# Attention scores of two head pairs in one visit of the matrix engine

## The chip, the cores and the metric

The kernel runs on one core of a Trainium2 chip. A core has a matrix engine (PE, TensorE), which also loads its stationary operands (PEld in the profile), a vector engine (DVE), an activation engine (ACT), a general engine (POOL) and a queue engine (SP). They run side by side and wait for one another by semaphores. [...] The metric is the device time of one run in microseconds (us). The kernel before took 494.76 us, the median of 3 runs (494.73 to 494.86).

## The reference

Attention over pooled keys and values feeds a small mixture of four experts. Eight batches of eight heads have 576 queries of 64 values each; eight neighbouring keys (and values) are averaged, so 72 remain.

```python
k_p = k.reshape(B, H, Sp, 8, D).mean(axis=3)          # Sp = 72
v_p = v.reshape(B, H, Sp, 8, D).mean(axis=3)
scores = scale * np.matmul(q, k_p.transpose(0, 1, 3, 2))
attn = exp(scores - max); attn /= attn.sum(-1)
x = np.matmul(attn, v_p)                              # -> rows of 512 values, one per query
for e in range(4):
    out += p[:, e] * (relu(x @ w1[e]) @ w2[e])         # 512 -> 1024 -> 512
```

Most of the arithmetic is in the last line: 4608 rows through four pairs of 512 x 1024 and 1024 x 512 products.

## The kernel before

**Chunks and tiles.** The first 512 queries of each batch make a chunk; the 64 left over from each of the eight batches make a ninth. A chunk and an expert make a tile. Chunk 0 is worked in a hand-written opening (`first_chunk`); the other 32 tiles run in one loop.

**Products.** The two expert products are not done by the textbook's eight block products of 2 x 2 blocks but by seven (sums and differences of blocks are formed on DVE ahead). `up_product` (line 642) does one of the seven of `x @ w1` for one of two halves of the hidden columns, called units; `down` (line 711) does one of the seven of `h @ w2`. A unit owns two PSUM banks. By the table at line 647, products 0, 2, 3 and 5 of a unit go to its bank 0, and products 1, 4 and 6 to its bank 1. Product 0 is also copied by ACT from bank 0 into bank 1 (line 673), where product 1 is added to it; the ReLU at line 677 then reads bank 1. From there until product 4, which starts a new sum, bank 1 is not used. Products 2 and 3 are copied by ACT from bank 0 to `partial` (line 675) before the next product is added on to bank 0. Products 4 and 6 are finished by DVE (line 640), and product 5 by ACT (line 681).

**The loop's slots.** The loop at line 1019 counts slots `g`. A slot issues, in this order: product `i` of unit 0; product `i - 1` of unit 1; the down product `i - 1` of the tile before; and then the attention pieces that were put at this slot. So each slot has 4 + 4 + 8 matrix products of 256 columns. The order written in the program is the order on each engine: nothing is rescheduled.

**The attention pieces.** While chunk `c` of the loop runs, the attention of a later batch is prepared. `pieces_later` (line 923) lists which piece stands after which slot; a batch has 28 slots, counted from the start of its four tiles. For the usual batch (3 to 7) the four `scores` pieces stand after slots -1, 3, 5 and 6, and for batch 2 (`plans[BUSY]`) after 11, 12, 13 and 15; batch 1 has its four in `first_chunk`. The `context` pieces (scores times values) come from slot 11 on (16 on for batch 2).

`scores` (line 363) works a pair of heads: four products, each with 64 contracted rows. The halves of the rows lie on partitions 0 to 63 and 64 to 127, so two of the products can run in the two halves of the matrix engine's rows at the same time, each into a bank of its own of the two-bank tile `att`. Then one ACT instruction takes the exponent of both banks, 72 x 1024 values (line 377). Batches below 2 alternate between `att` and a second tile, `att_first`, which is given up before the loop and becomes unit 0's banks. `rem_scores` (line 457) does the same for the 64 left-over queries, with 64-column products.

**Queues.** In the loop, ACT carries the copies and ReLUs of the up products, the exponents, the copy of the first down product (line 736), the scaling for POOL's additions (line 740), and for expert 0 also the first additions to the result (line 802). DVE carries the other additions (line 804), the block sums and the context's division. SP issues the transposing loads (queries, keys, context) and the stores.

Of the kernel before, what the change touches and what calls it, by code (L numbers as in the profile page):

```python
# [9 lines left out]
ACT = mybir.ActivationFunctionType  # L10
# [7 lines left out]
def kernel(  # L18
# [10 lines left out]
    nc = tc.nc  # L29
# [330 lines left out]

        return state[("kpT", b)][:].rearrange("p h j -> p (h j)")[lo:lo + D, h * SPT:h * SPT + P]

    def scores(b, pair):
        qT = state[("qT", b)]
        if pair == 0:
            state[("expT", b)] = apool.tile([SP, H, 2, 2, P], BF16, name="expT")
        expT = state[("expT", b)]
        sc_ps = two_banks(b)[:].rearrange("p a (h n) -> p a h n", h=2)
        for hh in range(2):
            h = 2 * pair + hh  # L370
            for r2 in range(2):
                lo = r2 * D
                nc.tensor.matmul(  # L373
                    sc_ps[:, r2, hh], lhsT=key_columns(b, h, lo), rhs=qT[lo:lo + D, h],
                    skip_group_check=True,
                )
        nc.scalar.activation(
            out=expT[:, 2 * pair:2 * pair + 2].rearrange("j h a b t -> j b (h a) t"),
            in_=sc_ps[0:SP].rearrange("j b h (a t) -> j b (h a) t", t=P),
            func=ACT.Exp, scale=EXP_SCALE,  # L380
        )

    def divide(c_ps, x_tok):

# [446 lines left out]
    def first_chunk():  # L831


        def each(*pieces):
            for piece in pieces:
                piece()

        sums = {e: first_weight_sums(e) for e in range(E)}

        def both(step):  # L840
            for unit in range(2):
                up_product(0, 2, unit, step)

        each(*(lambda n=n: x_sum(0, n) for n in range(4)), *sums[0][0:3])
        norm_probs()
        up(0, 1, (0, 1))
        hidden_sums(0, 0, 0)
        hidden_sums(0, 0, 1)
        up(0, 1, (2, 3))
        each(*sums[1][0:3])  # L850
        up(0, 1, (4,), bank=att_first[1][:, 1])
        each(sums[2][0], sums[2][1], sums[2][3], sums[2][2])
        up(0, 1, (5,), bank=chains[0])
        both(0)
        up(0, 1, (6,), bank=chains[1])
        both(1)
        up(0, 1, (7,), bank=chains[0])
        each(sums[0][3], sums[1][3], *weight_sums(0))
        both(2)
        down(0, 0, 0)  # L860
        hidden_sums(0, 0, 2)
        both(3)
        down(0, 0, 1)
        hidden_sums(0, 0, 3)
        both(4)
        down(0, 0, 2)
        both(5)
        down(0, 0, 3)
        both(6)
        load_w2(3)  # L870
        fold_keys(1)
        up(0, 3, (0,), bank=units[1][0])
        down(0, 0, 4)
        up(0, 3, (1, 2, 3))
        queries(1, 0)
        queries(1, 1)
        down(0, 0, 5)
        keys(1, every)
        queries(1, 2)
        down(0, 0, 6)  # L880
        scores(1, 0)
        queries(1, 3)
        turn_of("att", 2)
        up(0, 3, (4,))
        each(*sums[3][0:3])
        scores(1, 1)
        up(0, 3, (5,))
        scores(1, 2)
        up(0, 3, (6,))
        each(*weight_sums(1)[0:3])  # L890
        scores(1, 3)
        up(0, 3, (7,))
        fold_first, *fold_rest = values_folds(1)
        fold_first()
        down_plain(0, 1, 0)
        each(*fold_rest)
        load_wide(0, 0)
        load_q(2)
        load_wide(0, 1)
        load_wide(1, 0)  # L900
        load_wide(1, 1)
        load_q_rem(0)
        load_q_rem(1)
        load_wide(1, 2)
        down_plain(0, 1, 1)
        down_plain(0, 1, 2, range(0, 3))
        context(1, 0)
        down_plain(0, 1, 2, range(3, FCH))
        context(1, 1)
        turn(1, 0)  # L910
        down_plain(0, 1, 3)
        context(1, 2)
        turn(1, 1)
        down_plain(0, 2, 0)
        context(1, 3)
        turn(1, 2)
        down_plain(0, 2, 1)
        turn(1, 3)
        each(*weight_sums(3)[0:3])
        down_plain(0, 2, 2)  # L920
        each(*(lambda n=n: x_sum(1, n) for n in range(4)))

    def pieces_later():


        at = {}

        def put(slot, *pieces):
            at.setdefault(slot, []).extend(pieces)

        usual = dict(
            queries=-8, keys=-9, values=-2, scores=(-1, 3, 5, 6), contexts=(11, 14, 18, 21),
            q=1, k=(-2, 0, 5, 9), v=(-2, 0, 5, 9), x=(22, 25, 25, 25), rem=(-3, 17, 24, 25),
        )
        plans = {b: usual for b in range(BUSY, B + 1)}
        plans[BUSY] = dict(
            queries=0, keys=4, values=12, scores=(11, 12, 13, 15), contexts=(16, 18, 19, 21),
            q=6, k=(5, 8, 11, 14), v=(13, 16, 19, 26), x=(24, 25, 25, 25), rem=(0, 6, 8, 14),
        )
        plans[B] = dict(usual, x=(24, 24, 25, 25), rem=(-3, 17, 21, 22))  # L940
        plans[BUSY + 1] = dict(usual, keys=-8, values=4, v=(5, 8, 12, 16))

        for b, plan in plans.items():
            start = 7 * E * (b - BUSY)

            def put_each(what, pieces):
                for slot, piece in zip(plan[what], pieces, strict=True):
                    put(start + slot, piece)

            if b == BUSY:  # L950
                put(start + 1, lambda: fold_wide(0, 0))
                put(start + 4, lambda: fold_wide(0, 1))
                put(start + 5, lambda: load_q_rem(BUSY))
                put(start + 8, lambda: fold_wide(1, 0))
                put(start + 12, lambda: fold_wide(1, 1))
            if b < B:
                put(start + plan["queries"], lambda b=b: queries(b))
                put(start + plan["keys"], lambda b=b: fold_keys(b))
                put(start + plan["keys"] + (b > BUSY), lambda b=b: keys(b, every))
                put(start + plan["values"], *values_folds(b))  # L960
                put_each("scores", [lambda b=b, pair=pair: scores(b, pair) for pair in range(NPAIR)])

                for r, slot in zip((2, 3, 0, 1), plan["contexts"]):
                    put(start + slot, lambda b=b, r=r: context(b, r))
                    put(start + slot + 1, lambda b=b, r=r: turn(b, r))
            if b + 1 < B:
                put(start + plan["q"], lambda b=b: load_q(b + 1), lambda b=b: load_q_rem(b + 1))
                for what in range(2):
                    put_each("kv"[what], [lambda b=b, what=what, part=part: load_part(b + 1, what, part)
                                          for part in range(NR)])  # L970
            if b % 2 == 0:
                i = b // 2 - 1
                put_each("rem", [lambda i=i, do=do: do(i)
                                 for do in (rem_queries, rem_scores, rem_context, rem_turn)])
            put_each("x", [lambda b=b, n=n: x_sum(b, n) for n in range(4)])
        return at

    ENG = mybir.EngineType
    with tc.manual_schedule(
# [28 lines left out]


        N = len(order)  # L1010
        later = pieces_later()
        below_of = [(0, 3)] + order
        sums = {}
        for at, pieces in (((3,), weight_sums(3)[3:]), ((8,), weight_sums(1)[3:]), ((12, 15, 22, 14), weight_sums(2)),
                           ((15,), first_weight_sums(3)[3:])):
            for slot, piece in zip(at, pieces, strict=True):
                sums.setdefault(slot, []).append(piece)
        POOLED = (4,)
        for g in range(7 * N + 1):
            t, i = divmod(g, 7)  # L1020
            if i in (0, 2, 3) and t < N:
                hidden_sums(*below_of[t], i)
            if t < N:
                up_product(*order[t], 0, i)
            t2, i2 = divmod(g - 1, 7)
            if 0 <= t2 < N:
                up_product(*order[t2], 1, i2)
            if i == 1 and t < N:
                hidden_sums(*below_of[t], i)
            if g == 0:  # L1030

                down_plain(0, 2, NR - 1)
            else:
                down(*below_of[t2], i2, t2 % 2, POOLED)
            for piece in later.get(g, ()):
                piece()
            for piece in sums.get(g, ()):
                piece()
            if g == 7 * (N - 2):
                load_last_weights()  # L1040
# [29 lines left out]
```

## Time and profile before

| | |
|---|---|
| time, median of 3 runs | 494.76 us (494.73 to 494.86) |
| profiled execution | 494.84 us, of which 492.7 us from the first to the last instruction |
| granted clock of the matrix engine | 0.999 |
| PE busy | 485.5 us |
| PE weight loads | 408.4 us |
| DVE busy | 378.4 us |
| ACT busy | 305.5 us |
| POOL busy | 115.7 us |
| score products of `scores` | 112, in 28 visits of 4 |
| exponent of one pair, 72 x 1024 | 1020 ns |

The profile has one line per kind of instruction: its line of the kernel, the engine, what it writes and reads, how many there were, their total and mean time, and the idle time ahead of them with what ended it. [...] In a timeline each line has the start, the length, and how many equal instructions were merged into it.

### The profile page before, as it was taken

What the parts mean: (1) busy time and instruction counts of PE and PEld (TensorE: products, weight loads), DVE (VectorE), ACT (ScalarE), POOL (GpSimd) and SP (SyncE); (2) the same over time, 40 slices, a digit from 0 to 9 for tenths busy, and PEclk for the clock granted to TensorE, in tenths of its full rate; (3) what the DMA queues carried; (4) which work ended last, traced back from release to release, by engine and by line L of the source; (5) the groups of instructions that cost most, each with busy time, mean ns of one, the idle gap of its engine ahead of it and who ended that gap; (6) DMA issues with size and microseconds to landing.
All of it is one profiled execution on the core that took longest, in us unless ns stands there. A gap on an engine that the chain in (4) does not pass through costs nothing.

```text
span 492.7 us, 11536 instructions
## 1 busy us (share of the span) xinstructions
PE 485.5 (99%) x4695; PEld 408.4 (83%) x4701; DVE 378.4 (77%) x758; ACT 305.5 (62%) x569; POOL 115.7 (23%) x114
## 2 busy tenths in 40 slices
PE   8999999999999999999999999999999999999996
PEld 4867468788888888888889889888898888888885
DVE  5786889799668976798579876896678766876674
ACT  4876446856766568656765676557665566556650
POOL 8320323242432055015321352111011100010010
PEclk9999999999999999999999999999999999999999
DMA  9999999975887479344954397311111010004003
GB/s 199 212 206 203 197 172 127 107 79 69 98 118 63 79 77 144 35 79 44 162 59 84 31 151 76 68 26 44 56 23 23 23 65 1 13 21 86 1 1 87
DMA packets 101812, 41.97 MB, mean 85 GB/s; under 512 B 73840, under 2 KB 100208, under 8 KB 101760
## 3 DMA queue, kind: packets, MB, share of 16 engines
q0 software_dynamic: 56928, 22.42, 40.3%
q1 hardware_dynamic: 43728, 17.77, 16.5%
q10 hardware_dynamic: 1104, 1.05, 0.6%
q8 instruction: 37, 0.61, 0.5%
q14 instruction: 15, 0.12, 0.1%
HBM read 45.69 MB, written 9.44 MB: 112 GB/s over the span
## 4 chain that ended last, share of the span: by engine, by line
PE 98%; DVE 0%; ACT 0%; issue 0%
PE o_ps L728 41%; PE unit L660 41%; PE o_ps L754 3%; PE unit L582 2%; PE att L373 2%; PE att L427 1%; PE unit L787 1%; PE unit L326 1%; PE o_ps L582 1%; PE unit L597 1%; PE att_first L660 1%; PE o_ps L597 0%; PE att L481 0%; PE att L464 0%; PE unit L306 0%; PE att L353 0%
## 5 line engine op out<-in xcount | busy, mean ns | idle before, releaser
L804 DVE SCALAR_TENSOR_TENSOR acc<-o_ps,p_all,acc 128x256 f32<-128x256 f32 (+1 forms) x285 | 127.1, 486 | 52.6 <-PE o_ps L728 36.6
L728 PEld LDWEIGHTS <-H 128*128 128x128 bf16 x1320 | 129.0, 98 | 15.6 <-DMA w_bf<-in_moe_w_dram 0.6
L660 PEld LDWEIGHTS <-w_bf 128*128 128x128 bf16 x1056 | 100.9, 98 | 15.8 <-issue 3.6
L640 DVE CUSTOM_DVE_ANT_0 H<-unit,partial 128x512 bf16<-128x512 f32 x128 | 87.3, 685 | 26.1 <-PE unit L660 21.5
L728 PE MATMUL o_ps<-w_bf,H 128*128 128x256 bf16 x792 | 102.6, 273 | 0.3 <-ACT w_bf L675 0.3
L660 PE MATMUL unit<-xT,w_bf 128*128 128x256 bf16 x680 | 97.6, 273 | 0.0
L675 ACT COPY partial<-unit 128x512 f32<-128x512 f32 x128 | 72.0, 590 | 33.2 <-PE unit L660 33.0
L742 POOL TENSOR_TENSOR acc<-acc,addend 128x512 f32<-128x512 f32 x24 | 30.4, 1267 | 261.9 <-ACT addend L740 206.5
L660 PEld LDWEIGHTS <-wu_bf 128*128 128x128 bf16 x792 | 75.7, 98 | 10.7 <-issue 1.7
L660 PE MATMUL unit<-xs,wu_bf 128*128 128x256 bf16 x512 | 76.9, 273 | 0.0
L728 PE MATMUL o_ps<-wt_bf,H 128*128 128x256 bf16 x528 | 68.4, 273 | 0.0
L728 PEld LDWEIGHTS <-S 128*128 128x128 bf16 x528 | 51.7, 98 | 6.2
L681 ACT ACTIVATE H<-unit 128x512 bf16<-128x512 f32 x64 | 38.2, 597 | 29.5 <-PE unit L660 29.3
L677 ACT ACTIVATE H<-unit 128x512 bf16<-128x512 f32 x64 | 38.8, 606 | 27.9 <-PE unit L660 27.8
L673 ACT COPY unit<-unit 128x512 f32<-128x512 f32 x65 | 38.0, 584 | 15.4 <-PE unit L660 15.4
L660 PE MATMUL unit<-xs,w_bf 128*128 128x256 bf16 x256 | 38.5, 273 | 0.0
L802 ACT ACTIVATE acc<-o_ps,p_all 128x256 f32<-128x256 f32 x72 | 30.3, 473 | 11.0 <-PE o_ps L728 9.6
L151 POOL DMA_DIRECT2D kraw<-in_k_dram x20 | 26.4, 1319 | 37.2 <-DMA kraw<-in_k_dram 37.2
L660 PE MATMUL unit<-xT,wu_bf 128*128 128x256 bf16 x228 | 34.2, 272 | 0.0
L728 PE MATMUL o_ps<-w_bf,S 128*128 128x256 bf16 x264 | 34.2, 273 | 0.0
L728 PE MATMUL o_ps<-wt_bf,S 128*128 128x256 bf16 x264 | 34.2, 273 | 0.0
L151 POOL DMA_DIRECT2D vraw<-in_v_dram x20 | 29.2, 1462 | 17.6 <-DMA vraw<-in_v_dram 17.6
(168 smaller groups left out, 516.2 us busy)
## 6 DMA issues: line engine op xcount, KB each, us to landing
out_dram<-acc SPq DMA_DIRECT2D x32, 256.0 KB, 4.2
w_bf<-in_moe_w_dram POOLq DMA_DIRECT2D x7, 1024.0 KB, 21.9
q_sb<-in_q_dram POOLq DMA_DIRECT2D x7, 512.0 KB, 9.8
vraw<-in_v_dram POOLq DMA_DIRECT2D x22, 144.0 KB, 6.8
kraw<-in_k_dram POOLq DMA_DIRECT2D x21, 144.0 KB, 5.4
w_bf<-in_moe_w_dram POOLq DMA_DIRECT2D x2, 512.0 KB, 8.1
wt_bf<-in_k_dram POOLq DMA_DIRECT2D x4, 144.0 KB, 5.4
wt_bf<-in_v_dram POOLq DMA_DIRECT2D x4, 144.0 KB, 4.2
```

Source lines behind the costliest of these rows:

```text
L151: nc.gpsimd.dma_start(out=raw[:], in_=rows_of(src, b, 2 * part, 2 * part + 2), accum_op=ALU.add if part else ALU.bypass)
L582: nc.tensor.matmul(out_ps, lhsT=w1_bf[:, e, kc, fc * P:(fc + 1) * P], rhs=xT[:, kc, at], start=(kc == 0), stop=(kc == KC - 1), skip_group_ ...
L640: nc.vector._custom_dve(TENSOR_ADD_SAT, out=dst, in0=ps, in1=part, s0=LARGEST, s1=0.0)
L660: nc.tensor.matmul(ps[:, n * HN:(n + 1) * HN], lhsT=lhs[:, kc, f:f + P], rhs=rhs[:, kc, :], start=(not grows and n == 0 and kc == 0), stop ...
L673: nc.scalar.copy(out=banks[1][:], in_=ps)
L675: nc.scalar.copy(out=part[:, step - 2], in_=ps)
L677: nc.scalar.activation(out=quarter(0, 0), in_=ps, func=ACT.Relu)
L681: nc.scalar.activation(out=quarter(0, 1), in_=ps, func=ACT.Relu)
L728: nc.tensor.matmul(ps[:, j], lhsT=lhs[:, i, j * P:(j + 1) * P], rhs=rhs[:, i, :], start=(not grows and i == 0 and j == 0), stop=(i == HF - 1),
L742: nc.gpsimd.tensor_add(out=dst, in0=dst, in1=addend[:])
L802: nc.scalar.activation(out=dst, in_=o_ps, func=ACT.Copy, scale=prob)
L804: nc.vector.scalar_tensor_tensor(out=dst, in0=o_ps, scalar=prob, in1=dst, op0=ALU.mult, op1=ALU.add,)
```

## The change

`scores` is split into `score_products` (the four products, given two banks) and the exponent. A new piece, `scores_of_two`, issues the four products of one pair into `att` and straight after them the four of the next pair into bank 1 of unit 0 and bank 1 of unit 1. It then issues the exponents of that second pair, one ACT instruction of 72 x 512 values for each bank. The first pair's exponent, of 72 x 1024 values, is issued one slot later, after the two up products of that slot. In that later slot the two up products are issued in the reverse order, unit 1 first.

A usual batch has two such visits, after slots 2 and 9, in place of four of one pair each. Batch 2 has one after slot 9 and two of a single pair after slots 12 and 15. In the opening, batch 1's four `scores` pieces are put in two neighbouring couples, each still with one exponent per pair, and one product of expert 1 (`down_plain(0, 1, 0)`) is moved ahead of the second couple. One block sum of expert 2's weights moves from slot 12 to slot 10.

```diff
-    def scores(b, pair):
+    def score_products(b, pair, banks):
...
+    def scores(b, pair, part=None):
+        sc_ps = two_banks(b)
+        if part != 1:
+            score_products(b, pair, [sc_ps[:, r2] for r2 in range(2)])
+        if part == 0:
+            return
         nc.scalar.activation(
...
+    def scores_of_two(b, pair):
+        scores(b, pair, 0)
+        banks = [unit[1][:] for unit in units]
+        score_products(b, pair + 1, banks)
+        for r2 in range(2):
+            nc.scalar.activation(
+                out=state[("expT", b)][:, 2 * pair + 2:2 * pair + 4, :, r2].rearrange("j h a t -> j (h a) t"),
+                in_=banks[r2][0:SP].rearrange("j (h t) -> j h t", t=P),
+                func=ACT.Exp, scale=EXP_SCALE,
+            )
...
         down(0, 0, 6)
-        scores(1, 0)
         queries(1, 3)
-        turn_of("att", 2)
         up(0, 3, (4,))
         each(*sums[3][0:3])
+        scores(1, 0)
         scores(1, 1)
-        up(0, 3, (5,))
+        up(0, 3, (5, 6))
+        each(*weight_sums(1)[0:3])
+        down_plain(0, 1, 0)
+        fold_first, *fold_rest = values_folds(1)
+        fold_first()
         scores(1, 2)
-        up(0, 3, (6,))
-        each(*weight_sums(1)[0:3])
         scores(1, 3)
         up(0, 3, (7,))
-        fold_first, *fold_rest = values_folds(1)
-        fold_first()
-        down_plain(0, 1, 0)
...
         usual = dict(
-            queries=-8, keys=-9, values=-2, scores=(-1, 3, 5, 6), contexts=(11, 14, 18, 21),
+            queries=-8, keys=-9, values=-2, scores=((2, 2), (9, 2)), contexts=(11, 14, 18, 21),
...
         plans[BUSY] = dict(
-            queries=0, keys=4, values=12, scores=(11, 12, 13, 15), contexts=(16, 18, 19, 21),
+            queries=0, keys=4, values=12, scores=((9, 2), (12, 1), (15, 1)), contexts=(16, 18, 19, 21),
...
+                        put(start + slot, lambda b=b, pair=pair: scores_of_two(b, pair))
+                        put_amid(start + slot + 1, lambda b=b, pair=pair: scores(b, pair, 1))
...
-        for at, pieces in (((3,), weight_sums(3)[3:]), ((8,), weight_sums(1)[3:]), ((12, 15, 22, 14), weight_sums(2)),
+        for at, pieces in (((3,), weight_sums(3)[3:]), ((8,), weight_sums(1)[3:]), ((10, 15, 22, 14), weight_sums(2)),
...
+            ups = [(*order[t], 0, i)] if t < N else []
             if 0 <= t2 < N:
-                up_product(*order[t2], 1, i2)
+                ups.append((*order[t2], 1, i2))
+            for args in reversed(ups) if g in amid else ups:
+                up_product(*args)
+            if g in amid:
+                amid[g]()
```

More of the change, by code (lines that the diff above doesn't have):

```diff
@@ L366, in scores @@
             state[("expT", b)] = apool.tile([SP, H, 2, 2, P], BF16, name="expT")
-        expT = state[("expT", b)]
-        sc_ps = two_banks(b)[:].rearrange("p a (h n) -> p a h n", h=2)
         for hh in range(2):
@@ L373, in scores @@
                 nc.tensor.matmul(
-                    sc_ps[:, r2, hh], lhsT=key_columns(b, h, lo), rhs=qT[lo:lo + D, h],
+                    banks[r2][:, hh * HN:(hh + 1) * HN], lhsT=key_columns(b, h, lo), rhs=qT[lo:lo + D, h],
                     skip_group_check=True,
                 )
+    def scores(b, pair, part=None):
[4 more added lines that the diff above has]
+            return
         nc.scalar.activation(
-            out=expT[:, 2 * pair:2 * pair + 2].rearrange("j h a b t -> j b (h a) t"),
-            in_=sc_ps[0:SP].rearrange("j b h (a t) -> j b (h a) t", t=P),
+            out=state[("expT", b)][:, 2 * pair:2 * pair + 2].rearrange("j h a b t -> j b (h a) t"),
+            in_=sc_ps[0:SP].rearrange("j b (h t) -> j b h t", t=P),
             func=ACT.Exp, scale=EXP_SCALE,
         )
+    def scores_of_two(b, pair):
[8 more added lines that the diff above has]
+            )
     def divide(c_ps, x_tok):
@@ L923, in pieces_later, with put_amid @@
     def pieces_later():
-        at = {}
+        at, amid = {}, {}
+        def put_amid(slot, piece):
+            amid[slot] = piece
         def put(slot, *pieces):
@@ L960, in pieces_later @@
                 put(start + plan["values"], *values_folds(b))
-                put_each("scores", [lambda b=b, pair=pair: scores(b, pair) for pair in range(NPAIR)])
+                pair = 0
+                for slot, n in plan["scores"]:
+                    if n == 2:
+                        put(start + slot, lambda b=b, pair=pair: scores_of_two(b, pair))
+                        put_amid(start + slot + 1, lambda b=b, pair=pair: scores(b, pair, 1))
+                    else:
+                        put(start + slot, lambda b=b, pair=pair: scores(b, pair))
+                    pair += n
                 for r, slot in zip((2, 3, 0, 1), plan["contexts"]):
@@ L975, in pieces_later @@
             put_each("x", [lambda b=b, n=n: x_sum(b, n) for n in range(4)])
-        return at
+        return at, amid
     ENG = mybir.EngineType
@@ L1010 @@
         N = len(order)
-        later = pieces_later()
+        later, amid = pieces_later()
         below_of = [(0, 3)] + order
         sums = {}
-        for at, pieces in (((3,), weight_sums(3)[3:]), ((8,), weight_sums(1)[3:]), ((12, 15, 22, 14), weight_sums(2)),
+        for at, pieces in (((3,), weight_sums(3)[3:]), ((8,), weight_sums(1)[3:]), ((10, 15, 22, 14), weight_sums(2)),
                            ((15,), first_weight_sums(3)[3:])):
@@ L1022 @@
                 hidden_sums(*below_of[t], i)
-            if t < N:
-                up_product(*order[t], 0, i)
             t2, i2 = divmod(g - 1, 7)
+            ups = [(*order[t], 0, i)] if t < N else []
             if 0 <= t2 < N:
-                up_product(*order[t2], 1, i2)
+                ups.append((*order[t2], 1, i2))
[3 more added lines that the diff above has]
+                amid[g]()
             if i == 1 and t < N:
```

## The prediction

> **What bounds the kernel now.** I read the page's busy line, then its chain of work.
>
> ```profile
> PE 485.5 (99%) x4695; PEld 408.4 (83%) x4701; DVE 378.4 (77%) x758; ACT 305.5 (62%) x569; POOL 115.7 (23%) x114
> ...
> PE 98%; DVE 0%; ACT 0%; issue 0%
> ```
>
> The chain that ended last is PE work for 98% of the span. Whatever takes time off PE's own sequence shortens the run; whatever is saved on ACT or DVE alone does not; a new wait of PE lengthens it one for one. But a busy PE hides gaps of a few hundred ns[...], so I asked for the score products' line.
>
> ```profile
> L373 PE MATMUL att<-qT,kpT x104: 269/274/281, 49.5 to 343.0; 64*128 64x256 bf16 x104
> ...
>   issue: 6.5, 28
> ```
>
> In 28 visits the weight-load half of PE sat idle for 6.5 us, 0.23 us each, waiting for nothing that the profile shows. To see why, narrow windows of the timeline around one visit (start, length, number merged):
>
> ```profile
> 336.62 0.27 PE L728 MATMUL o_ps<-wt_bf,S 128*128 128x256 bf16 x1
> ...
> 336.82 0.28 PE L373 MATMUL att<-qT,kpT 64*128 64x256 bf16 x2
> ...
> 336.94 0.27 PE L373 MATMUL att<-qT,kpT 64*128 64x256 bf16 x2
> ...
> 337.14 0.28 PE L660 MATMUL unit<-xs,wu_bf 128*128 128x256 bf16 x1
> ```
>
> The last ordinary product starts at 336.62, two score products together at 336.82, two more at 336.94, the next ordinary one at 337.14. Ordinary products follow at 0.11 us (the eight down products of that slot start from 335.85 to 336.62: 0.77 / 7). So a visit costs 0.52 - 0.11 = 0.41 us: about 0.10 going in, 0.22 for two couples, 0.10 coming out. That a longer visit does not pay the ends again is seen at the 64-row visit for the left-over queries:
>
> ```profile
> 80.23 0.27 PE L728 MATMUL o_ps<-w_bf,H 128*128 128x256 bf16 x1
> ...
> 80.44 0.41 PE L464 MATMUL att<-qTr,kpT 64*128 64x64 bf16 x16
> 80.78 0.39 PE L660 MATMUL unit<-xT,w_bf 128*128 128x256 bf16 x2
> ```
>
> Again 0.21 going in; then eight couples of 64 columns in 0.41 - 0.19 = 0.22 us of starts, 0.03 us apart.
>
> Last, ACT around slot 9 of batch 7, the densest place, with PE's end of that slot and the context that follows:
>
> ```profile
> 347.43 0.59 ACT L675 COPY partial<-unit 128x512 f32<-128x512 f32 x1
> 348.17 0.60 ACT L677 ACTIVATE H<-unit 128x512 bf16<-128x512 f32 x1
> 348.75 0.84 ACT L802 ACTIVATE acc<-o_ps,p_all 128x256 f32<-128x256 f32 x2
> 349.48 1.07 ACT L675 COPY partial<-unit 128x512 f32<-128x512 f32 x2
> 350.44 0.85 ACT L802 ACTIVATE acc<-o_ps,p_all 128x256 f32<-128x256 f32 x2
> 351.32 0.59 ACT L675 COPY partial<-unit 128x512 f32<-128x512 f32 x1
> ...
> 347.62 1.04 PE L728 MATMUL o_ps<-w_bf,H 128*128 128x256 bf16 x8
> ...
> 351.99 0.42 PE L427 MATMUL att<-vp,expT 72*128 72x65 bf16 x8
> ```
>
> ACT is nearly without a pause there: its 62% is an average, and this is where a new wait would come from.
>
> [...] The trace has 1020 for the 1024-column exponent and 590 to 606 for 512-column copies and ReLUs.
>
> **The change part by part.**
>
> *Visits (PE).* The number of products stays. 28 visits become 15: batch 1 from 4 to 2, batch 2 from 4 to 3, batches 3 to 7 from 4 to 2 each. Each of the 13 merges saves one pair of ends: two visits cost 2 x 0.41 = 0.82 us; a merged one 0.41 + 2 x 0.11 = 0.63. The unrounded starts make it 0.20 us. 13 x 0.20 = 2.6 us, all on PE, all on the chain.
>
> *Exponents (ACT).* 11 merges in the loop turn two of 1020 ns into one of 1020 and two of 72 x 512, not in the trace. Below: half the long one, 0.51 us. [...] I take 0.60, the row of the 512-column ReLU, and 0.50 from start to start when they follow each other (two L675 copies take 1.07 us). That is 11 x 0.1 us more on ACT, nothing by itself.
>
> *Where they stand.* I walk through slots 9 to 13 of a usual batch, counting from the start of the slot's last down product (the eight above end at 348.66, the last started 0.27 before: 348.39). Score couples start at 0.21, 0.33, 0.43, 0.54; the next up product at 0.75. ACT: the two L802 end at 1.20 (349.59); the bank exponents run 1.10 to 1.70 and 1.60 to 2.20; unit 1's copy of product 2 ends at 2.69, unit 0's copy of product 3 at 3.17, the `att` exponent at 4.09, the next two L802 at 4.85, unit 1's copy of product 3 at 5.34. PE, if it never waits, asks for these:
> - unit 1's bank 1, free after its ReLU: at 0.43. That ends at 0.13 as a rule (in slot 2 of this batch the ReLU ends at 335.01 and the last down product starts at 334.87: 0.14), but at 0.38 here (348.77). Margins 0.29 and 0.05.
> - unit 0's product 4 at 2.49, after the first bank exponent (1.70): margin 0.79.
> - unit 1's product 3 at 2.93, after the copy of product 2 (2.69): margin 0.24. In the usual order its copy would stand second, 0.5 us later, and PE would wait.
> - the context after slot 11 at 4.24, after the `att` exponent (4.09): margin 0.15.
> - down product 4 of slot 12 at 5.4, after the L802 of slot 10 (4.85): margin 0.5.
>
> PE to ACT a semaphore takes about 0.08 us here (a product ending at 347.35 is followed by L675 at 347.43); the same the other way leaves every margin but the 0.05 positive, that one short by 0.03 us once. Slot 2 has no L802 on ACT (its down product belongs to expert 3, which DVE adds), so it is easier: product 3's margin is 0.45, and no context follows. In batch 2 the same sum gives 0.25 as its smallest margin; `att` is free there at 85.87, when the DVE division of slot 8 ends, and wanted at 86.6, and the keys, issued by SP at 79.87 and landing in at most 5.1 us, are there by 85.0.
>
> *What is queued behind the new waits.* A late ACT delays PE's in-order queue, hence everything; DVE's final sums of product 4 wait for `partial`, with half a microsecond to spare. Neither SP's nor POOL's order changes. Block sum 12 to 10: 0.68 us of DVE where it idles 1.33 us (87.67 to 89.00); no cost.
>
> *Opening.* Two merges, counted above. `down_plain(0, 1, 0)` now runs at about 51.4 instead of 53.3; its weights are there (DVE reads them at 51.22). Its addition moves ahead of the first fold of the values, which before waited until 53.85 for its DMA and ended with the folds at 57.10, just ahead of the context (57.41). By the same durations the folds now end at 56.6 and the context is asked for at 57.0: no wait.
>
> *Sum.* 2.6 us less, some 0.05 to 0.1 us back at the tight margins. The sum is against the 492.7 us span; that execution took 494.84 us as a run, among 494.73 to 494.86, so I carry the difference over: 494.76 - 2.55 = 492.2 us.
>
> **Rivals.**
> *A, as above:* 492.2 (491.8 to 492.6).
> *B, part is lost:* the bank exponents or the semaphores are slower than taken, and the context after slot 11 and product 3 in slots 4 and 11 wait a little. 0.1 us at each of 11 merged visits takes 1.1 us: 493.3. For it: margins of 0.15 and 0.24. Against: ACT's durations vary by a few ns.
> *C, no gain:* the ends are paid again where the visit passes from `att` to the units' banks, or at the product that waits for the ReLU. Then 0.20 x 13 come back: 494.8. For it: no visit in the trace mixes two tiles. Against: visits whose first product also waits for ACT show the same 0.20.
> *D, slower:* the two bank exponents, ahead of unit 1's copy of product 2, take as long as the long one[...]: 0.8 us more per visit. Less the margin of 0.24 (0.45 in slot 2), PE waits about 0.45 us at product 3, 11 x 0.45 = 5, less 2.6: 497.2. It ends slower from 0.24 us of waiting per merged visit on. Against: no 512-column row of ACT that I read takes over 0.63 us.
>
> **How the numbers follow.** A 0.80, B 0.09, C 0.06, D 0.05. The predicted time is A's. 491.7 to 493.3 holds A and most of B. A measurement tells 0.2% (1.0 us) from no change; A and B lie beyond it (faster 0.88), C within, with a sliver of B (0.07), D beyond it on the other side (0.05).
>
> **What the profile after would show.** Right: 112 score products in 15 visits, the idle "issue" time of their weight loads near 15 x 0.23 = 3.5 us; in a merged visit four couples and 0.75 us from the last down product to the next up product; ACT with 17 long and 22 short exponents, the short near 0.6 us; no idle time of PE ahead of the context or of unit 1's product 3. Wrong: a second gap of 0.1 us inside a visit (C); PE waiting for the exponent or copy lines of ACT (B, D).

## The result, and the profile after

| | before | after |
|---|---|---|
| time, median of 6 runs of each, side by side | 494.75 us (494.47 to 494.86) | 492.52 us (491.92 to 493.61) |
| ratio | | 0.9957 [0.9944, 0.9970] |
| span of the profiled execution | 492.7 us | 490.8 us |
| start of PE's last product in that execution | 487.92 us | 485.11 us |

The change is faster by 0.43%, 2.2 us. The six runs of the kernel before lie within 0.4 us; those of the changed kernel spread over 1.7 us. Their spans, from the first to the last instruction, spread over 1.0 us (489.8 to 490.8): the slowest, 493.61 us, has a span of 490.7, 2.9 us less, where the other five are 2.0 to 2.1 us longer than their spans.

The page after, engines and chain (busy time, share of the span, instructions; then shares of the chain that ended last):

```profile
PE 482.6 (98%) x4701; PEld 410.0 (84%) x4701; DVE 377.0 (77%) x758; ACT 304.3 (62%) x580; POOL 116.1 (24%) x114
...
PE 92%; DMA 4%; POOL 2%; issue 0%; DVE 0%; POOLq 0%
```

PE is still the bound. Read the 92% with care: DMA and POOL are in the chain because in this execution one down product of the opening waited 0.50 us for the last weights, and the chain then follows that transfer back. A share of the chain says which way it was followed, not how much was lost there. ACT has 11 instructions more (580 for 569), one per merged visit of the loop.

The score products' line after (count, shortest / median / longest ns, first and last start, shape; below it the idle time of the engine and its weight loads ahead of them):

```profile
L371 PE MATMUL att<-qT,kpT x60: 269/274/280, 49.0 to 345.3; 64*128 64x256 bf16 x60
L371 PE MATMUL unit<-qT,kpT x44: 269/269/269, 86.4 to 345.5; 64*128 64x256 bf16 x44
L371 PE MATMUL att_first<-qT,kpT x8: 269/269/269, 49.3 to 53.5; 64*128 64x256 bf16 x8
...
  issue: 3.6, 15
```

60 + 44 + 8 are the same 112 products. 44 of them now write a unit's bank: the second pair of 11 visits. The weight loads were idle ahead of 15 visits for 3.6 us, 0.24 us each, instead of 28 visits for 6.5 us.

One merged visit, in narrow windows of the timeline (start, length, equal instructions merged):

```profile
344.93 0.27 PE L746 MATMUL o_ps<-w_bf,H 128*128 128x256 bf16 x1
345.14 0.28 PE L371 MATMUL att<-qT,kpT 64*128 64x256 bf16 x2
...
345.26 0.27 PE L371 MATMUL att<-qT,kpT 64*128 64x256 bf16 x2
...
345.37 0.27 PE L371 MATMUL unit<-qT,kpT 64*128 64x256 bf16 x2
...
345.47 0.27 PE L371 MATMUL unit<-qT,kpT 64*128 64x256 bf16 x2
345.68 0.28 PE L678 MATMUL unit<-xs,wu_bf 128*128 128x256 bf16 x1
```

An ordinary product of 256 columns is recorded with 0.27 us while the next one starts 0.109 us after it, so the pace is read from the starts of neighbouring products. The way in is paid once (344.93 to 345.14), then four couples about 0.11 us apart, then the way out (345.47 to 345.68). The two products of a couple, one in each half of the rows, start 3 to 4 ns apart. Going from `att` to the units' banks (345.26 to 345.37) costs no more than going on in `att`. In the single records all 11 merged visits of the loop have the same starts to within 2 ns: 205, 325, 434 and 543 ns after the last down product, the next up product at 748 ns, where a single visit took 530. Two singles beyond their ordinary steps cost 2 x (530 - 109) = 842 ns, one merged 748 - 109 = 639. That is 0.20 us per merge.

The densest place, ACT in slot 9 of batch 7 and after:

```profile
344.45 0.61 ACT L695 ACTIVATE H<-unit 128x512 bf16<-128x512 f32 x1
345.29 0.84 ACT L820 ACTIVATE acc<-o_ps,p_all 128x256 f32<-128x256 f32 x2 [0.22 <-ACT H L695]
346.02 1.07 ACT L395 ACTIVATE expT<-unit 72x512 bf16<-72x512 f32 x2
346.98 1.07 ACT L693 COPY partial<-unit 128x512 f32<-128x512 f32 x2
347.92 1.05 ACT L382 ACTIVATE expT<-att 72x1024 bf16<-72x1024 f32 x1
348.83 0.86 ACT L820 ACTIVATE acc<-o_ps,p_all 128x256 f32<-128x256 f32 x2
```

and PE over the same stretch:

```profile
347.44 0.60 PE L678 MATMUL unit<-xs,wu_bf 128*128 128x256 bf16 x4
347.87 0.60 PE L678 MATMUL unit<-xT,w_bf 128*128 128x256 bf16 x4
348.31 1.04 PE L746 MATMUL o_ps<-wt_bf,H 128*128 128x256 bf16 x8
349.18 0.42 PE L445 MATMUL att<-vp,expT 72*128 72x65 bf16 x8
349.44 0.60 PE L678 MATMUL unit<-xT,wu_bf 128*128 128x256 bf16 x4
```

The two short exponents run 346.02 to 347.09 and the two `partial` copies end at 348.05. Unit 1's copy of product 2 is the first of these two and ends about 0.48 us earlier, ahead of unit 1's product 3 at 347.87. The long exponent ends at 348.97; the context asks at 349.18. PE waited for neither: its products start at their ordinary steps (347.44 + 0.44, + 0.44, + 0.87 us for the eight down products, so 349.18). That no line carries a bracket would not be enough, for a wait of 0.2 us can go without one, as an experiment below shows.

The last two lines show which products pay the ends of a visit. The context's eight have 72 contracted rows, also fewer than 128, and pay nothing: the first starts one ordinary step after the last down product (349.07 + 0.11), and the next up product follows 0.26 us later, eight of their own steps of 0.033 us. The context of the left-over queries differs in that its products run two at a time, in two halves of the array's columns (72*64 in the line):

```profile
321.09 0.27 PE L746 MATMUL o_ps<-wt_bf,S 128*128 128x256 bf16 x1
...
321.29 0.45 PE L499 MATMUL att<-vp,expTr 72*64 72x65 bf16 x16
...
321.67 0.28 PE L678 MATMUL unit<-xs,wu_bf 128*128 128x256 bf16 x1
```

It has 0.20 us going in, like the score products, and its eight couples take 0.38 us to the next product where eight steps are 0.26. So here the ends came with products that share the array in halves, of the rows or of the columns, and not with fewer rows as such.

The exponents by tile (columns as for the score products):

```profile
L395 ACT ACTIVATE expT<-unit x22: 583/591/596, 87.0 to 346.5; 72x512 bf16<-72x512 f32 x22
L382 ACT ACTIVATE expT<-att x15: 1010/1042/1054, 49.6 to 347.9; 72x1024 bf16<-72x1024 f32 x15
...
L382 ACT ACTIVATE expT<-att_first x2: 1010/1014/1017, 50.5 to 54.5; 72x1024 bf16<-72x1024 f32 x2
```

17 long, 22 short.

**Where the time went.** Lining the two traces up at the same products, PE's last product starts 2.81 us earlier: 0.42 comes from the opening, 0.21 from batch 2, and 0.42 from each of batches 3 to 7, that is 0.21 for each of 13 merges (2.75), and 0.05 from weights that landed sooner in the opening. The span shrank by 1.9 only. The rest is in the tail, after PE's last product: 5.71 us to the end of the span, 4.74 before. The DMA view of the changed kernel has, between 487.2 and 488.3, a queue that was not there in the tail before (packets, MB, share of the 16 engines), and the last two stores, issued at 485.94, with their time from issue to landing:

```profile
q8 instruction: 1, 0.02, 5.4%
...
out_dram<-acc SPq DMA_DIRECT2D x1, 128.0 KB, 3.5
out_dram<-acc ACTq DMA_DIRECT2D x1, 128.0 KB, 3.8
```

A block of 16 KB of instructions was fetched at 487.28, while the last stores ran; the stores took 3.5 and 3.8 us, where the kernel before, with its last such block at 486.38, has 2.5 and 2.8. That these blocks are PE's instructions is my estimate: PE's products and weight loads are 9402 of the 11549 instructions in the trace (81%), and this queue moved 0.61 of the 0.73 MB of the two instruction queues (83%). That the fetch slowed the stores is inferred from the times: of the six profiles for which this document gives the time of the last such block, no other has it among the last stores, and the other five have a tail of 4.71 to 4.74 us. The other five executions of the changed kernel had spans of 489.8, 489.9, 490.1, 490.7 and 490.8 us: some show the whole 2.8, some lose up to 1 us of it.

### The profile page after: what moved, and what is told of

It reads as the page before. It is cut to its first block, busy times and chain, and to the rows that moved or that the text cites. A ratio compares the mean times of both kernels' runs of the same rounds, so it can differ in the third digit from the quotient of the medians.

```text
span 490.8 us, 11549 instructions
## 1 busy us (share of the span) xinstructions
PE 482.6 (98%) x4701; PEld 410.0 (84%) x4701; DVE 377.0 (77%) x758; ACT 304.3 (62%) x580; POOL 116.1 (24%) x114
## 4 chain that ended last, share of the span: by engine, by line
PE 92%; DMA 4%; POOL 2%; issue 0%; DVE 0%; POOLq 0%
PE o_ps L746 41%; PE unit L678 41%; DMA w_bf<-in_moe_w_dram 4%; PE o_ps L772 3%; PE unit L600 1%; PE att L445 1%; PE unit L805 1%; POOL wt_bf L141 1%; PE att L371 1%; POOL w_bf L206 1%; PE unit L371 0%; PE att_first L678 0%; PE att L499 0%; PE att L482 0%; POOL p_all L226 0%; PE unit L463 0%
## 5 line engine op out<-in xcount | busy, mean ns | idle before, releaser
L678 PEld LDWEIGHTS <-w_bf 128*128 128x128 bf16 x1056 | 102.1, 98 | 12.9 <-DMA w_bf<-in_moe_w_dram 0.3
```

The lines of the kernel that those rows point to most:

```text
L678: nc.tensor.matmul(ps[:, n * HN:(n + 1) * HN], lhsT=lhs[:, kc, f:f + P], rhs=rhs[:, kc, :], start=(not grows and n == 0 and kc == 0), stop ...
```

## The experiments

The theory: a visit's two ends cost 0.20 us, the change saves 13 of them, and ACT keeps up because the short exponents come first. The rivals: the gain is elsewhere (in the opening's new order, or in the moved pieces); or ACT eats part of it. Each group of kernels shares its runs of the kernel before: its median was 494.80 us beside the first four, 494.77 beside the next four and 494.93 beside the last three. Times are medians with their range and number of runs; the ratio has its 95% interval in brackets and need not be that of the two medians. A diff shows the run against the changed kernel, unless the text says otherwise.

**The opening alone.** Batch 1's two merges with their new order; the loop is the one of the kernel before, of which the diff shows the two lines of the plans.

```diff
-            queries=-8, keys=-9, values=-2, scores=((2, 2), (9, 2)), contexts=(11, 14, 18, 21),
+            queries=-8, keys=-9, values=-2, scores=(-1, 3, 5, 6), contexts=(11, 14, 18, 21),
...
-            queries=0, keys=4, values=12, scores=((9, 2), (12, 1), (15, 1)), contexts=(16, 18, 19, 21),
+            queries=0, keys=4, values=12, scores=(11, 12, 13, 15), contexts=(16, 18, 19, 21),
```

> Only the opening is changed: batch 1's four visits become two, the loop is as before. If the gain is the saved ends of the visits (the theory), two merges save 2 x 0.21 us of PE time: the loop's first down product starts 0.4 to 0.5 us earlier, the time is 494.3 against 494.75. Rival, the opening is held by its weight transfers and nothing comes of it: 494.7 to 494.8, and the loop starts where it did. The end of the run (last matrix product's start to the end of the span) should be as before, 4.7 us[...].

Measured: 494.32 us (493.98 to 495.18, 21), ratio 0.9989 [0.9983, 0.9996]. PE's last product starts at 487.50, 0.42 earlier than before. This is two merges' worth, and no more: the reordered opening pays nothing else and costs nothing else.

**The loop alone.** Its complement: the opening as before.

```diff
         queries(1, 2)
         down(0, 0, 6)
+        scores(1, 0)
         queries(1, 3)
+        turn_of("att", 2)
         up(0, 3, (4,))
         each(*sums[3][0:3])
-        scores(1, 0)
         scores(1, 1)
-        up(0, 3, (5, 6))
...
+        up(0, 3, (5,))
...
```

> Only the loop is changed, the opening is as before. Theory: 11 merges x 0.21 us, the last matrix product starts 2.3 us earlier than before (485.6 for 487.9). As a time 492.4 if the end of the run is as long as before, up to 1.0 us more (493.4) if the last fetch of PE instructions falls among the last stores, as in the profile of the change[...]. Rival, the gain comes from somewhere else than the visits (the opening's new order): less than 1 us here.

Measured: 492.47 us (492.34 to 493.17, 5), ratio 0.9953 [0.9939, 0.9966]. PE's last product starts at 485.94, 1.97 earlier than before, in an execution in which the weights of the opening held PE 0.36 us longer than in the profile before: 2.33 without that, 0.21 for each of 11 merges. The medians add up as well: 0.48 from the opening and 2.33 from the loop.

**The same exponents, two visits again.** In batches 3 to 7 the first pair's products are issued one step earlier, ahead of the down product; ACT's work and its order stay as changed. Only the merging is undone.

```diff
     def scores_of_two(b, pair):
-        scores(b, pair, 0)
+        if b == BUSY:
+            scores(b, pair, 0)
...
+                        if b > BUSY:
+                            early[start + slot] = lambda b=b, pair=pair: scores(b, pair, 0)
...
+            if g in early:
+                early[g]()
```

> As the change, but in batches 3 to 7 the first pair's products are issued one step earlier in the same slot, ahead of the down product, so that each merged visit is two visits again; exponents, banks, slots and the order of the up products stay. Theory (the ends of a visit are what is saved): 10 merges are undone, 10 x 0.21 = 2.1 us come back, the last matrix product starts at 487.2 against 485.1 of the change; time 494.0 to 494.8. Rival (the gain comes from the new slots, or from the shorter exponents leading): time as the change, 492 to 493.

Measured: 494.51 us (494.12 to 496.85, 13), ratio 1.0000 [0.9990, 1.0011]. The gain is gone. PE's last product starts at 487.52, 0.40 earlier than before: three merges stay, less a small loss named below. In the profile of this kernel the score products' line has, of their weight loads:

```profile
  issue: 5.7, 25
```

25 visits for 15, 5.7 us for 3.6, and in batches 3 to 7 every visit steps 530 ns again. This is the experiment that ties the time to the visits: the short exponents, the units' banks and the new order of the up products all stay, and without the merge they gain nothing. The ten undone merges cost 0.42 - 0.21 = 0.21 us each. About 0.05 us more per batch went after slot 11, where the context now waits for the `att` exponent (in batch 3 that ends at 142.77 and the context starts at 142.82).

**The up products of the following slot in their usual order.** The change swaps unit 0 and unit 1 in a slot after a merged visit.

```diff
-            for args in reversed(ups) if g in amid else ups:
+            for args in ups:
```

> As the change, but the two up products of the slot after a merged visit stand in the usual order, unit 0 first. By the walk through the slots the copy of unit 1's product 2 then starts 0.5 us later and PE, which had 0.24 us to spare after slot 9 and 0.45 after slot 2, waits for it: about 0.3 us in six visits and 0.1 in five, 2.5 us in all. Theory: 494.5 to 495.2, PE shows waits for the copy line. Rival, the margins are larger than worked out (semaphores or copies faster): no wait, 492 to 493. Rival, the order doesn't matter[...]: the same, 492 to 493.

Measured: 493.85 us (493.08 to 495.28, 9), ratio 0.9980 [0.9969, 0.9990], so 1.3 us of the change's gain is lost by the medians and 1.37 us on PE in the profile; expected was 2.5. The timeline of slot 9, batch 7 (starts late by what was lost earlier):

```profile
348.12 1.07 ACT L693 COPY partial<-unit 128x512 f32<-128x512 f32 x2
...
348.59 0.60 PE L678 MATMUL unit<-xs,wu_bf 128*128 128x256 bf16 x4
...
349.25 0.60 PE L678 MATMUL unit<-xT,w_bf 128*128 128x256 bf16 x4
```

The copies end at 349.19 and unit 1's product starts at 349.25; at PE's step of 0.44 us it would have started at 349.03. So PE waits 0.22 us, though its line has no bracket, and it does in each of the six slot-9 visits (1.3 us in all); after slot 2 it waits nowhere. The swap is a part of the change that is needed, but my walk made ACT late by some 0.1 us too much. Two sizes behind that: a semaphore from ACT to PE took 0.06 us here where I had 0.08, and two short ACT instructions follow each other at 0.48 us where I had 0.50.

**The long exponent first.** Both pairs' products in one visit, but the 1024-value exponent of the first pair is issued at once, ahead of the bank exponents.

```diff
     def scores_of_two(b, pair):
-        scores(b, pair, 0)
+        scores(b, pair)
...
-            if g in amid:
-                amid[g]()
```

> As the change, but the 1024-column exponent of the first pair is issued at once, ahead of the two 512-column ones of the second pair, in place of one slot later. Theory (PE's waits follow from ACT's queue): after slot 9 the first bank exponent ends 0.9 us later (2.6 for a need at 2.5) and the copy of unit 1's product 2 about 0.9 later (3.6 for a need at 2.9), so PE waits some 0.75 us in six visits; after slot 2 some 0.35 us in five; 6 us in all: 497.5 to 499. Rival (ACT's order is of no weight, its mean load of 62% absorbs it): 492 to 493.

Measured: 496.74 us (496.51 to 497.89, 5), ratio 1.0041 [1.0028, 1.0054]: slower than before the change, if less so than expected (497.5 to 499). Slot 9 of batch 7 in this kernel:

```profile
350.28 1.01 ACT L382 ACTIVATE expT<-att 72x1024 bf16<-72x1024 f32 x1
...
350.82 1.04 PE L746 MATMUL o_ps<-wt_bf,S 128*128 128x256 bf16 x8
...
351.18 1.08 ACT L395 ACTIVATE expT<-unit 72x512 bf16<-72x512 f32 x2
...
351.82 0.60 PE L678 MATMUL unit<-xs,wu_bf 128*128 128x256 bf16 x4
...
352.13 1.08 ACT L693 COPY partial<-unit 128x512 f32<-128x512 f32 x2
...
352.78 0.60 PE L678 MATMUL unit<-xT,w_bf 128*128 128x256 bf16 x4 [0.36 <-ACT partial L693]
```

and the waits of PE that its waits table has at the top (total us, times, longest):

```profile
PE unit L678 <- ACT partial L693: 2.1, 6, 0.4
```

Everything behind the long exponent on ACT comes 0.9 us later, and PE waits twice. Unit 0's product 4 needs the bank that the first bank exponent reads until about 351.77: the eight down products' steps of 0.11 us end at 351.69, and it starts at 351.82 (no bracket; the starts show it). Unit 1's product 3 would follow 0.44 us later, at 352.26, and waits for its copy until 352.78. (The table's 0.36 us each count from the recorded end of the product before, so they are less than the 0.52 by the starts.) That is 0.65 us for each slot-9 visit and 0.20 for each slot-2 visit, 4.9 us in the profile for the 6 expected. This is the mechanism of the forecast's rival D: the mean of these waits is 0.45 us per visit, the price that D put on an ACT 0.8 us late. That the merge would not pay with bank exponents as long as D supposed is inferred from this; such exponents were not run.

**What disturbs the gain.** The remaining runs ask why the changed kernel spreads over 1.7 us. About 0.8 us of its slowest run lie outside the span, which no profile covers; what follows bears on the other 1.0 us. First, eight more PE instructions at the start, to move the last fetch of instructions away from the last stores, if the blocks are PE's:

```diff
+        idle(4, units[1][0][:], P)
```

> As the change, with four small matrix products (8 PE instructions) added in the opening, ahead of PE's wait for the first queries, where PE waits for a transfer afterwards anyway. Tail theory: in the profile of the change the last 16 KB fetch of PE instructions starts at 487.3, after PE's last work, among the last stores, which land 1.0 us late; in the one before, with 4 PE instructions more, it starts at 486.4, ahead of PE's end. With 9426 PE instructions it should again start before PE's last product, the end of the run should take 4.7 us for 5.7, and the times should gather at 491.8 to 492.1 in place of 491.9 to 493.6. Rival (stores simply land late at times, or the opening's transfers vary): median 492.3 to 492.7 with the same spread.

Measured: 492.58 us (491.63 to 494.19, 6), ratio 0.9956 [0.9942, 0.9969]. The fetch came 1.3 us ahead of PE's last product and the tail was 4.71 us, as expected. But the times spread as before, and this profile shows another loss, of a key transfer that is late in batch 2 (DVE, then ACT, then PE wait one after the other; the brackets give the idle time and what ended it):

```profile
109.35 0.76 DVE L285 TENSOR_TENSOR kp<-kraw 72x512 bf16<-72x512 bf16 x2 [0.59 <-DMA kraw<-in_k_dram]
...
111.23 0.86 DVE L823 SCALAR_TENSOR_TENSOR acc<-o_ps,p_all,acc 128x256 f32<-128x256 f32 x2
...
112.19 0.57 ACT L755 COPY o_ps<-o_ps 128x512 f32<-128x512 f32 x1 [0.21 <-DVE acc L823]
...
112.81 0.81 PE L747 MATMUL o_ps<-w_bf,H 128*128 128x256 bf16 x6 [0.18 <-ACT o_ps L755]
```

PE lost 0.49 us there.

The counterpart, with its diff against the kernel before: that kernel with four PE instructions fewer, as many as the changed kernel has, which by the same theory should bring its fetch among its last stores.

```diff
-        idle(13)
+        idle(11)
```

> The kernel before[...]; nothing else differs. Tail theory: the last fetch of PE instructions moves past PE's last product, into the last stores, and the end of the run takes up to 1.0 us longer: runs between 494.7 and 496, a spread of about 1 us where the kernel before has 0.3. Rival (the tail of the change has another reason): 494.6 to 494.9, as before.

Measured: 494.57 us (494.47 to 495.24, 13), ratio 0.9997 [0.9989, 1.0005]. The fetch did not come late (486.25), and the tail was 4.73 us. So the number of PE instructions does not set it in the way I thought; that theory falls. The change itself, run again, had it at 483.74 with its tail at 4.74 us, and in the kernel with the usual order of the up products it came at 491.79, after the last instruction, where it met no store (tail 4.74). So one program fetches early or late; a fetch among the last stores was seen in the one profile of the change alone.

Next, batch 2's last two visits merged as well, with the eight instructions of the first of these runs:

```diff
-            queries=0, keys=4, values=12, scores=((9, 2), (12, 1), (15, 1)), contexts=(16, 18, 19, 21),
+            queries=0, keys=4, values=12, scores=((9, 2), (16, 2)), contexts=(18, 19, 20, 21),
```

> As e6_fetch_early, and batch 2's last two visits (slots 12 and 15) are merged into one at slot 16, with its contexts moved to slots 18, 19, 20 and 21. Theory: one more merge, 0.21 us less than e6_fetch_early, 491.6 to 491.9, if the contexts in four slots running find the bank free. Rival: contexts in neighbouring slots wait for the division of the one before on DVE, 0.5 us or more slower than e6_fetch_early.

Measured: 492.03 us (491.82 to 492.31, 5), ratio 0.9942 [0.9930, 0.9954]. The merge saved its 0.2 us, but 0.38 was lost ahead of the down product of slot 23:

```profile
110.50 0.86 DVE L823 SCALAR_TENSOR_TENSOR acc<-o_ps,p_all,acc 128x256 f32<-128x256 f32 x2
...
111.46 0.57 ACT L755 COPY o_ps<-o_ps 128x512 f32<-128x512 f32 x1 [0.21 <-PE unit L679]
...
112.08 1.03 PE L747 MATMUL o_ps<-w_bf,H 128*128 128x256 bf16 x8 [0.19 <-ACT o_ps L755]
```

It is the same place as in the run with the late keys, with another origin: the fold of the keys now stands behind the later context's division on DVE, so DVE's sums end at 111.36, and ACT's copy starts at 111.46. Its bracket names a product of PE; but it starts 0.10 us after DVE's sums, as it does in the run with the late keys, where the bracket names DVE. So the fold of batch 3's keys stands too close here. Moving it two slots later, in the change itself:

```diff
-        plans[BUSY + 1] = dict(usual, keys=-8, values=4, v=(5, 8, 12, 16))
+        plans[BUSY + 1] = dict(usual, keys=-6, values=4, v=(5, 8, 12, 16))
```

> As the change, but batch 3's keys are folded on DVE two slots later (slot 22 of batch 2 in place of 20), and transposed a slot after that. Theory of the spread: in e6_fetch_early DVE stood 0.59 us ahead of that fold until the last transfer of the keys had landed (109.33), and PE lost 0.49 us two slots on, behind DVE's sum and ACT's copy; the change runs into it in some executions because PE comes there earlier (landing 106.4 to 109.3, wanted at 108.6). With two slots (3.5 us) more this wait can't occur: the median comes down to 491.9 to 492.2 and no run lies above 493. Rival (the opening's weight transfers, first down product between 33.3 and 34.1, or the last stores make the spread): median and spread as the change, 492.3 to 492.6, 491.6 to 494.

Measured: 492.57 us (491.87 to 493.28, 6), ratio 0.9947 [0.9934, 0.9960]. The spread did not shrink, so the key transfer is not its main cause.

Both edits together, the fold three slots later (`keys=-5`) and batch 2 merged twice:

> As the change, with batch 2's last two visits merged at slot 16 (contexts at 18, 19, 20, 21), and batch 3's keys folded three slots later, clear of these contexts. In e8_batch2_merged PE lost 0.38 us behind the fold that met a context's division on DVE; here it shouldn't. Theory: one more merge of 0.21 us without that loss, 0.2 us under e9_keys_later: 491.6 to 492.0. Rival: the contexts in four slots running cost something themselves, no less than e9_keys_later.

Measured: 491.92 us (491.68 to 493.11, 6), ratio 0.9939 [0.9927, 0.9952]. In its profile PE goes through slot 23 without a wait (its down product at 111.92), and the extra 0.2 us is there.

And beside these two, the change unaltered:

> The change itself, unaltered, for its spread beside the two others on the same chip. Both theories: median 492.1 to 492.7, runs from 491.8 to 493.6.

Measured: 491.88 us (491.73 to 492.63, 6), ratio 0.9937 [0.9925, 0.9950], tail 4.74 us; 492.1 to 492.7 was expected. So of the three the change itself is as good as the version with one merge more: 0.21 us is below what these runs tell apart. Over both of its groups, 12 runs, the change has a median of 492.1 us.

**What stays open.** The change ran at 0.9957 and at 0.9937 of the kernel before, in two groups of runs. Three things were seen to take a part in single executions: the instruction fetch among the last stores (1.0 us, inferred), the key transfer (0.49 us on PE), and the landing of the opening's weights (the product that waits for them started between 33.35 and 34.07 us in the profiled executions). Two of them were aimed at, and neither edit made the spread smaller. The kernel before spreads too in the later groups (494.27 to 496.43). What decides in which execution they strike was not found, nor how much of the spread they explain.

## Why the prediction was right, point by point

- **The visit's ends.** Right in place and size: 0.21 us per merge seen (0.20 taken), 13 merges, 2.75 us on PE. What the 0.10 us at an end consists of was not shown. The two halves of the change add up, and undoing the merge alone takes the gain away. Rival C's second gap between `att` and the units' banks was not there: the step is 0.11 us, the ordinary one.
- **Count of visits and idle time of the weight loads.** 15 visits and 3.6 us; 15 and 3.5 were forecast.
- **Exponents.** 17 long and 22 short. The short one takes 583 to 596 ns (0.60 taken), the long one 1042 in the middle (1010 to 1054) where I took 1020: both harmless, though the long one varied by 44 ns and not by the few that were held against rival B.
- **The walk through slots 9 to 13.** Right in its verdict, PE waits nowhere for ACT. Its margins were slightly too small: the context had 0.21 us (0.15 forecast), the ReLU ahead of unit 1's bank, for which 0.05 us was left at worst, ended 0.14 us after the last down product's start as in the walk's ordinary case, and with the usual order of the up products PE waited 0.22 us where the walk gives 0.3, and after slot 2 not at all. The failed term is the chain of ACT instructions, overestimated by 0.06 to 0.1 us over four of them. The forecast deducted 0.05 to 0.1 us for tight margins; no such loss was seen.
- **Order as the condition.** Rival D's price per visit (0.45 us of waiting) was not met with short exponents first; with the long one first PE lost 0.65 and 0.20 us per visit, 0.45 in the mean, and the kernel became slower than before. What separates gain from loss here is which exponent ACT does first.
- **The opening.** No wait at the context, 0.42 us for two merges.
- **From PE to the end of the run.** The forecast carried PE's gain over to the time one for one. PE gained 2.81 us in the profile, but the six runs gained 2.2 in the middle, inside the range, and the second six 3.05. The forecast time, 492.2, lies between the medians of these two groups (492.52 and 491.88); that it is as close as 0.3 us to the first is in part luck. The step that was too simple is this last one: it left out that transfers running beside PE land differently from execution to execution (the product that waits for the opening's weights started between 33.35 and 34.07 us; late keys cost PE 0.49 us in one execution; a tail with a fetch of instructions among its stores was 1.0 us longer, by inference because of it) and can hand part of a gain of this size back.

## What to carry to other kernels

Where small products that run side by side in halves of the array are scattered among large ones, count visits, not products: each visit here cost 0.2 us at its ends (the 72-row context, which runs one product at a time, cost none), and its two ends were hidden inside an engine that the profile before shows as 99% busy, visible only in the starts of neighbouring products and in the idle time of the weight loads. Merging visits asks for more free banks at once and makes the consumer's work come in one lump, so walk the consumer's queue and put first what the next product on the bound engine waits for; here that order alone made over 4 us. A gain of half a per cent is checked at PE's last product, since the tail and the transfers added up to 1 us in a single execution here.

## What the runs showed of the hardware

- Blocks of 16 KB came on a DMA queue that the profile names instruction (37 packets, 0.61 MB); that they are PE's instructions is an estimate from PE's share of the instructions, 81%. One that came during the last stores went with stores that took 1.0 us longer than before (3.5 and 3.8 us, for 2.5 and 2.8). It was seen in one of the six profiles with a time given for it; that the fetch was the cause is inferred from the time at which it ran. The same program had it at 487.3 in one execution and at 483.7 in another.
- Two products in the two halves of the rows (64*128) started 3 to 4 ns apart, and so did two in the two halves of the columns (72*64, 3 to 4 ns).
- The 0.10 us at either end of a visit were paid by products that share the array in halves (64*128: 205 ns from the last ordinary product to the first of the visit; 72*64: 203 ns), and not by products of 72 rows that run one at a time (72*128: 109 ns).
- Score couples into `att` and into the units' banks followed each other at 109 ns, like ordinary products of the same width; only the second couple of a visit came later, at 120 ns.
- The way from ACT's end to PE's start was 0.06 us where PE was waiting for it, and two 512-column ACT instructions started 0.48 us apart though each is recorded with 0.59. Likewise two 256-column products started 109 ns apart though each is recorded with 273.
